# VectorE's copy of the first group's k, ordered ahead of the second pair's reciprocal

## The chip, the cores and the metric
The kernel runs on one core of a Trainium2 chip. The metric is the time of one execution on the device in microseconds (us); less is better.

## What is computed
Three layers follow each other; the changed code is in the first, a gated linear attention over 4 batches, 8 heads, 768 positions and 48 dimensions:

```python
for t in range(S):
    state = alpha[:, :, t, :, None] * state + np.einsum('bhd,bhe->bhde', k[:, :, t], v[:, :, t])
    y[:, :, t] = np.einsum('bhd,bhde->bhe', q[:, :, t], state)
```

Its output, as 3072 tokens of 384 values, goes to a mixture of 8 experts (each token goes to one expert by a greedy order of its logits, at most 384 tokens to an expert; a hidden layer of 1024 with relu), and from there to a gated feed-forward layer of 1536 (`silu(x w_gate) * (x w_val)`, then `w_out`).

## The kernel before
Attention works on four pairs of heads (`p` = 0 to 3). Positions are cut into 12 chunks of 64, and two chunks of a pair make a group, so that a pair has 6 groups and the whole has 24 (`n`; the "first group" is n = 0).

`prep(p)` prepares a pair. It multiplies 32 factors of alpha in a tree (L126, L131, L135; on VectorE for the first two pairs, on GpSimd for the last two), takes the reciprocal of the product (L137), and derives the first factors from it: `rq` (L139), the last slot of g (L142) and the first of f (L143), with a memset of `ab` for the pair after next (L134) beside them. Then a chain of 31 products on VectorE (L166, the "FG steps") fills the tile FG with running factors, eight to a slice. After each slice of eight steps VectorE multiplies them with q (L171) and k (L172). TensorE transposes the results (L187), ScalarE writes them as the high half of q or k (L190), TensorE subtracts that half (L192), and ScalarE writes the low half (L194). So a pair's `qT` and `kT` are complete when the last of its L194 is. The transpose of `ab` (L146) and its copy (L148) give the decay between chunks. FG, qx and kx have one buffer each and are shared by all pairs; `qT` and `kT` have two. The loads of a later pair's q and k (L45) and alpha (L42) go out as soon as the slice before them is used up.

For each group, `sA(n)` copies that group's k from `kT` into one of two buffers `kBD` (two copies on VectorE, L205, one for each head of the pair; of them the change takes the second), starts a DMA on SyncE that transposes it into `kn` (L208), and brings v into halves (L211 on ScalarE, L216 on ScalarE, L217 on GpSimd). `sB` multiplies k with q (L227), masks (L229), subtracts and masks again (L231, L232). `sC` multiplies the transposed k with v (L241) and carries the state from chunk to chunk (L252 on TensorE, L257 on VectorE); it writes the state's two halves (L271 on ScalarE, L272 on GpSimd) and copies v into place (L276 on VectorE). `sD` forms the output (L287), `sE` sends it out (L306 to L313). With two `kBD` buffers, the copy for group n + 2 waits until the transposing DMA and the products of group n have read theirs.

The code is written group by group, but that is not the order on the engines. A scheduler with a timeline of its own places every instruction; `after(a, b)` is the way to tell it that a is to stand behind b. It adds a dependency that only orders, without a semaphore:

```python
    def after(a,b):
        tc.add_manual_dep(a.ins,b.ins.name,mybir.DependencyInfo(mybir.DependencyClass.NoSync,mybir.DependencyReason.DATA),reason="the first pair first")
```

The loads of weights for the last layer are unpacked on VectorE (L655, L657, L659) at the end of attention, in the router and in the first expert. DMAs are issued by SyncE, in order, on eight semaphores in turn, so that each waits for the one issued eight before it.

Of the kernel before, what the change touches and what calls it, by code (L numbers as in the profile page):

```python
# [22 lines left out]
B,H,S,D=4,8,768,48  # L23
# [7 lines left out]
def attention(ctx, tc, q, k, v, alpha, w_gate, xd, RP, MW, side, R):  # L31

    nc=tc.nc
# [24 lines left out]
    def load_v(m):  # L58
        if m>=NP*G//VG: return
        p,w=divmod(m,G//VG)  # L60
        vx[m]=P2.tile([128,VG*GC,B,D],F32,name="vx",tag="vx",bufs=VB)
        for h in range(2):
            for b in range(B):
                nc.sync.dma_start(vx[m][64*h:64*h+64,:,b],
                    bass.AP(tensor=v.tensor,offset=v.offset+(((b//2*2+h)*H+2*p+b%2)*S+w*VG*GC*C)*D,ap=[[D,C],[C*D,VG*GC],[1,D]]))
# [50 lines left out]
            nc.vector.tensor_copy(RI[64*h:64*h+48,48*h:48*h+48],ident[64*h:64*h+48,64*h:64*h+48])  # L116
        cst['wgh']=wgh; cst['RI']=RI

    fq={}
    def after(a,b):  # L120
        tc.add_manual_dep(a.ins,b.ins.name,mybir.DependencyInfo(mybir.DependencyClass.NoSync,mybir.DependencyReason.DATA),reason="the first pair first")
    def prep(p,first=False):
# [6 lines left out]
        n=8  # L129
# [3 lines left out]
        ab=P2.tile([XP,2,64],F32,name="ab")  # L133
        nc.vector.memset(ab,1.0)  # L134
        te.tensor_tensor(ab[:,:,0:D],tr[:,:,0],tr[:,:,1],op=OP.mult); yield  # L135
        inv=P2.tile([XP,2,D],F32,name="inv")
        nc.vector.reciprocal(inv,ab[:,:,0:D])  # L137
        rq=P2.tile([XP,2,D],F32,name="rq")
        nc.vector.tensor_scalar(rq,inv,par[:XP,1:2],par[:XP,0:1],op0=OP.mult,op1=OP.add)  # L139
        f=FG[:,0].rearrange("p j h d -> p h j d")[:,:,:,0:D]  # L140
# [57 lines left out]
    def sA(n):  # L198
        p,g=divmod(n,G)
        kb=kBD[n%NBD]; vb=vBD[n%2]  # L200
        for h in range(2):
            r=slice(64*h,64*h+48)

            o=kb[r].rearrange("p l (b c) h s -> p (l b) c h s",b=B)[:,:,:,h]; x=kT[p][r].rearrange("p l b g c s -> p (l b) g c s")[:,:,g]
            nc.vector.tensor_copy(o,x)  # L205

        kn[n]=P2.tile([128,2,U,128],F16,name="kn")
        nc.sync.dma_start_transpose(kn[n].rearrange("p l u x -> p (l u) x"),kb.rearrange("p l u h s -> p (l u h s)"))  # L208
        if g%VG==0:
            vg=vx[n//VG]  # L210
            ii=nc.scalar.activation(vg,vg,AF.Copy,scale=SX)  # L211
            if VD and p==0: after(ii,chain[0])
        vt=vx[n//VG][:,g%VG*GC:(g%VG+1)*GC].rearrange("p c b d -> p b c d")
        vh[n]=P2.tile([128,2,U,D],F16,name="vh",tag="vh",bufs=3)
        vu=vh[n].rearrange("p l (b c) d -> p l b c d",b=B)
        nc.scalar.activation(vu[:,0],vt,AF.Copy)  # L216
        nc.gpsimd.tensor_tensor(vu[:,1],vt,vu[:,0],op=OP.subtract)  # L217
        if g%VG==VG-1: load_v(n//VG+VB)
        yield
        yield  # L220
# [113 lines left out]
    for _ in prep(0,True): pass  # L334
    late()
    ready=[0]
    def preps():
        for p in range(1,NP):
            yield from prep(p)
            ready[0]=p  # L340
    cur=preps()
    for i in range(-2,NG+2):

        if 0<=i+2<NG:
            while ready[0]<(i+2)//G: next(cur,None)
        gens=[]
        if 0<=i<NG: gens.append((sC(i),6))
        if 0<=i+1<NG: gens.append((sB(i+1),2))
        if 0<=i-1<NG: gens.append((sD(i-1),3))
        if 0<=i-2<NG: gens.append((sE(i-2),3))  # L350
        if 0<=i+2<NG: gens.append((sA(i+2),2))
        if i+2>=PS0: gens.append((take(cur,PW),PW))
        if SIDE and SS<=i+2<SE: gens.append((take(side,SIDE),SIDE))
        merge(gens)
        if i==NG-RC: R.consts()
# [521 lines left out]
def full(tc,q,k,v,alpha,wg,w1,w2,wg2,wv2,wo2,out):  # L877
    nc=tc.nc
    with ExitStack() as top:
        D=top.enter_context(tc.tile_pool(name="dr",bufs=1,space=bass.MemoryType.DRAM))  # L880
        xd=D.tile([24*128,2,384],F16,name="xd")
        PT=top.enter_context(tc.tile_pool(name="rps",bufs=1,space=PS))
        R=Router(top,tc)
        MW=top.enter_context(tc.tile_pool(name="mw",bufs=1))
        M=Moe2Weights(tc,MW,wg2,wv2,wo2)
        side=M.load()
        with ExitStack() as ctx: L=attention(ctx,tc,q,k,v,alpha,wg,xd,PT,MW,side,R)
        with ExitStack() as ctx:
            R.start(ctx,L,PT)
            ffn(ctx,tc,xd,w1,w2,M,MW,out,R,side)  # L890
# [28 lines left out]
```

## Time and profile before

| | us |
|---|---|
| median of 3 runs | 980.42 |
| the three runs | 979.54, 980.69, 980.42 |
| the profiled execution | 981.15 |
| its span, first to last instruction | 979.4 |

| engine | busy us | share of the span |
|---|---|---|
| TensorE, matrix products | 827.0 | 84% |
| VectorE | 678.1 | 69% |
| ScalarE | 413.8 | 42% |
| GpSimd | 328.1 | 33% |

The profile names TensorE PE, VectorE DVE, ScalarE ACT, GpSimd POOL and SyncE SP (SPq where it issues DMAs). A row of a timeline gives the start in us from the span's start, the duration in us, engine, line, operation, tile written and tiles read, the count of instructions merged into the row, and, where the engine was idle before it, for how long and what ended that. Busy shares are averages over stages with different limits; a stage is read from its own rows.

### The profile page before, as it was taken

Reading aid. Unit: us, or ns where it says so; the run is one execution under the profiler, and the core shown is the slowest. Engines: PE = TensorE matmul, PEld = TensorE weight load, DVE = VectorE, ACT = ScalarE, POOL = GpSimd, SP = SyncE. Lnnn points to the kernel's source line nnn. Section 1 sums busy time; section 2 is a strip of 40 time slices with the busy share of each in tenths; the row PEclk is TensorE's granted clock in tenths of the full one; section 3 lists DMA queues with packets and bytes.
Section 4 is the critical chain, followed back from the end, with each engine's and each line's share of the span. In section 5 each row is a group of like instructions: output and inputs, shape, how many; then the busy total and the mean of one; then the engine's idle time right before and its main releaser. Section 6 shows DMA issues by size and latency. Waiting matters only on the chain. (4 is left out here: it accounts for less than half of the span.)

```text
span 979.4 us, 18512 instructions
## 1 busy us (share of the span) xinstructions
PE 827.0 (84%) x7216; PEld 529.9 (54%) x7216; DVE 678.1 (69%) x1856; ACT 413.8 (42%) x768; POOL 328.1 (33%) x308
## 2 busy tenths in 40 slices
PE   1657788877616778889999999999999998999997
PEld 0446567756413444556656656656655664666664
DVE  7869999749798997756865875774884687232130
ACT  5627576776505543432432342251343245332130
POOL 0153534426304544512431350360342246221231
PEclk9769898998855998999999999999999999999999
DMA  9996877879614440700420250070060038000000
GB/s 182 173 168 140 179 151 126 140 152 195 149 44 156 149 129 1 189 14 1 132 71 1 86 117 1 1 194 9 1 181 21 1 123 234 23 1 1 25 1 24
DMA packets 148055, 90.28 MB, mean 92 GB/s; under 512 B 121344, under 2 KB 138752, under 8 KB 147968
## 3 DMA queue, kind: packets, MB, share of 16 engines
q1 hardware_dynamic: 144896, 79.67, 35.5%
q0 software_dynamic: 3072, 9.44, 3.0%
q8 instruction: 56, 0.92, 0.4%
q14 instruction: 31, 0.25, 0.1%
HBM read 62.94 MB, written 9.44 MB: 74 GB/s over the span
## 5 line engine op out<-in xcount | busy, mean ns | idle before, releaser
L805 POOL TENSOR_TENSOR pTa<-pp,pTa 128x384 f16<-128x384 f32 x64 | 59.6, 932 | 258.6 <-ACT pTa L804 258.4
L766 PE MATMUL ph<-xT,w1s 128*128 128x384 f16 x576 | 103.6, 335 | 13.5 <-ACT o L816 10.1
L800 DVE TENSOR_TENSOR sg<-sg,pg 128x384 f32<-128x384 f32 x96 | 52.7, 549 | 77.0 <-ACT sg L799 76.9
L813 PE MATMUL po<-ma,pTa 128*128 128x384 f16 x576 | 104.0, 329 | 2.3 <-ACT pTa L804 2.3
L778 PE MATMUL px<-hT,w2s 128*128 128x384 f16 x576 | 97.0, 326 | 3.3 <-DVE hT L768 1.9
L766 PEld LDWEIGHTS <-w1s 128*128 128x128 f16 x576 | 56.3, 100 | 53.2 <-issue 20.7
L778 PEld LDWEIGHTS <-w2s 128*128 128x128 f16 x576 | 55.8, 98 | 40.0 <-issue 3.8
L796 PEld LDWEIGHTS <-mb 128*128 128x128 f16 x576 | 55.2, 98 | 40.5 <-issue 4.9
L813 PEld LDWEIGHTS <-pTa 128*128 128x128 f16 x576 | 55.6, 98 | 38.7 <-ACT pTa L804 2.4
L796 PEld LDWEIGHTS <-mc 128*128 128x128 f16 x576 | 55.8, 98 | 36.8 <-issue 1.2
L796 PEld LDWEIGHTS <-ma 128*128 128x128 f16 x576 | 55.4, 98 | 35.7
L804 ACT ACTIVATE pTa<-pp 128x384 f16<-128x384 f32 x64 | 33.3, 522 | 88.4 <-DVE pp L803 88.4
L799 ACT ACTIVATE sg<-pg 128x384 f32<-128x384 f32 x96 | 46.6, 486 | 53.1 <-PE pg L796 50.7
L803 DVE SCALAR_TENSOR_TENSOR pp<-sg,pv 128x384 f32<-128x384 f32 x96 | 52.9, 551 | 17.9 <-PE pv L796 13.5
L711 POOL TENSOR_TENSOR w2s<-stage,w2s 128x768 f16<-128x768 f32 x32 | 56.4, 1767 | 24.9 <-ACT stage L710 24.5
L796 PE MATMUL pg<-x,mb 128*128 128x384 f16 x288 | 57.8, 326 | 4.5 <-DVE sg L800 2.5
L805 POOL TENSOR_TENSOR pTb<-pp,pTb 128x384 f16<-128x384 f32 x32 | 30.0, 938 | 87.8 <-ACT pTb L804 87.8
L217 POOL TENSOR_TENSOR vh<-vx,vh 128x384 f16<-128x384 f32 x24 | 24.6, 1030 | 100.4 <-ACT vh L216 82.2
L796 PE MATMUL pv<-x,mb 128*128 128x384 f16 x288 | 57.7, 326 | 0.0
L166 DVE TENSOR_TENSOR FG<-FG,al 96x192 f32<-96x192 f32 x124 | 52.9, 437 | 2.1
L796 PE MATMUL pv<-x,mc 128*128 128x384 f16 x288 | 53.2, 331 | 0.0
L796 PE MATMUL pg<-x,mc 128*128 128x384 f16 x288 | 52.7, 326 | 0.0
(246 smaller groups left out, 1864.9 us busy)
## 6 DMA issues: line engine op xcount, KB each, us to landing
stage<-in_moe_w_dram SPq DMA_DIRECT2D x32, 384.0 KB
stage<-in_moe_w_dram SPq DMA_DIRECT2D x23, 512.0 KB
al<-in_alpha_dram SPq DMA_DIRECT2D x16, 288.0 KB
vx<-in_v_dram SPq DMA_DIRECT2D x64, 72.0 KB
xd<-xr SPq DMA_DIRECT2D x24, 192.0 KB
words<-in_moe_w_gate_dram SPq DMA_DIRECT2D x9, 512.0 KB
words<-in_moe_w_val_dram SPq DMA_DIRECT2D x9, 512.0 KB
words<-in_moe_w_out_dram SPq DMA_DIRECT2D x9, 512.0 KB
```

The costliest lines, as they stand in the source:

```text
L166: chain[p]=nc.vector.tensor_tensor(fg(j,HB-1-j),fg(j-1,HB-j),aa(j,HB-j),op=OP.mult)
L217: nc.gpsimd.tensor_tensor(vu[:,1],vt,vu[:,0],op=OP.subtract)
L711: behind(nc.gpsimd.tensor_tensor(dst[1],s,dst[0],op=OP.subtract),lo_after)
L766: mm(ps,lhsT=a[:,l,k,f*128:(f+1)*128],rhs=x[:,r,k],start=i==0,stop=i==8); i+=1
L778: mm(ps,lhsT=b[:,l,f,d*128:(d+1)*128],rhs=hT[:,r,f],start=i==0,stop=i==23); i+=1
L796: mm(ps,lhsT=w[:,l,k,f%4*128:(f%4+1)*128],rhs=x2[:,r,k],start=i==0,stop=i==8); i+=1
L799: nc.scalar.activation(sg,pg,AF.Sigmoid,scale=2.0**-16)
L800: nc.vector.tensor_tensor(sg,sg,pg,op=OP.mult)
L803: nc.vector.scalar_tensor_tensor(p,sg,2.0**-13,pv,op0=OP.mult,op1=OP.mult)
L804: nc.scalar.activation(pT[e][f//4][:,0,f%4],p,AF.Copy)
L805: nc.gpsimd.tensor_tensor(pT[e][f//4][:,1,f%4],p,pT[e][f//4][:,0,f%4],op=OP.subtract)
L813: mm(po,lhsT=pT[e][f//4][:,l,f%4,t*128:(t+1)*128],rhs=M.o[f//4][:,r,f%4],start=i==0,stop=i==35); i+=1
```

## The change
The copies of `sA` are kept by group number, and the reciprocal of the second pair (p = 1) gets an ordering dependency: it is to stand behind the first group's copy (the second of its two, on the same engine).

```diff
-    fq={}
+    fq={}; kc={}
...
-        nc.vector.reciprocal(inv,ab[:,:,0:D])
+        ri=nc.vector.reciprocal(inv,ab[:,:,0:D])
+        if p==1 and 0 in kc: after(ri,kc[0])
...
-            nc.vector.tensor_copy(o,x)
+            kc[n]=nc.vector.tensor_copy(o,x)
```

Behind line 137 every line number of the changed kernel is one higher. The scheduler places all that follows anew. Three places of that:

VectorE before, from the end of the second pair's tree (L135) to the third group's copy; kBD_135 and kBD_136 are the two buffers, ah are masked products of groups:

```order
L135 TENSOR_TENSOR ab<-tr 96x2x48
L137 RECIPROCAL inv<-ab 96x96
L139 TENSOR_SCALAR rq<-inv,par 96x96
L142 TENSOR_SCALAR FG<-inv,par 96x2x48
L134 MEMSET ab 96x128
L143 TENSOR_TENSOR FG<-al,rq 96x2x48
L205 COPY kBD_135<-kT 48x16x64 x2
L205 COPY kBD_136<-kT 48x16x64 x2
L166 TENSOR_TENSOR FG<-FG,al 96x2x2x48 x3
L229 TENSOR_TENSOR ah<-pA,mask 128x512
L166 TENSOR_TENSOR FG<-FG,al 96x2x2x48 x2
L229 TENSOR_TENSOR ah<-pA,mask 128x512
```

The rows that follow before are one more L166, an L232 and the third group's copy. The same stretch with the change, to the third group's copy:

```order
L206 COPY kBD_135<-kT 48x16x64 x2
L137 RECIPROCAL inv<-ab 96x96
L206 COPY kBD_136<-kT 48x16x64 x2
L140 TENSOR_SCALAR rq<-inv,par 96x96
L143 TENSOR_SCALAR FG<-inv,par 96x2x48
L134 MEMSET ab 96x128
L230 TENSOR_TENSOR ah<-pA,mask 128x512
L144 TENSOR_TENSOR FG<-al,rq 96x2x48
L167 TENSOR_TENSOR FG<-FG,al 96x2x2x48
L230 TENSOR_TENSOR ah<-pA,mask 128x512
L167 TENSOR_TENSOR FG<-FG,al 96x2x2x48
L233 TENSOR_TENSOR ah<-pA,mask 128x512
```

The first group's two copies stand ahead of the reciprocal, the second group's behind it, and two FG steps instead of six stand ahead of the third group's copy.

TensorE before, where the transposes of the second pair's first slice stand (L187; r and pY belong to the groups' output):

```order
L231 LDWEIGHTS negs
L231 MATMUL pA<-ah,negs 128x512
L187 MATMUL pt<-rid,FG 128x96 x8
L293 LDWEIGHTS negs
L293 MATMUL pY<-yh,negs 128x512
```

And with the change, the same transposes (now L188), 162 rows further on:

```order
L288 LDWEIGHTS sBD_140
L288 MATMUL pY<-qT,sBD_140 128x64
L288 LDWEIGHTS sBD_140
L288 MATMUL pY<-qT,sBD_140 128x64
L288 LDWEIGHTS sBD_140
L288 MATMUL pY<-qT,sBD_140 128x64
L188 MATMUL pt<-rid,FG 128x96 x8
```

They have moved behind products of the second group's output, which read that group's state halves (sBD_140).

VectorE before, at the first copies of the second pair (its first two groups):

```order
L276 COPY vBD_138<-vh 64x16x48 x2
L166 TENSOR_TENSOR FG<-FG,al 96x2x2x48 x7
L171 TENSOR_TENSOR FG<-qx,FG 96x2x8x48
L205 COPY kBD_135<-kT 48x16x64 x2
L205 COPY kBD_136<-kT 48x16x64 x2
L172 TENSOR_TENSOR FG<-kx,FG 96x2x8x48
```

And with the change:

```order
L277 COPY vBD_138<-vh 64x16x48 x2
L172 TENSOR_TENSOR FG<-qx,FG 96x2x8x48
L173 TENSOR_TENSOR FG<-kx,FG 96x2x8x48
L167 TENSOR_TENSOR FG<-FG,al 96x2x2x48 x8
L206 COPY kBD_135<-kT 48x16x64 x2
L206 COPY kBD_136<-kT 48x16x64 x2
L172 TENSOR_TENSOR FG<-qx,FG 96x2x8x48
L173 TENSOR_TENSOR FG<-kx,FG 96x2x8x48
```

The product with q that stood directly ahead of the copies now stands directly behind them.

## Rows read from the trace of the kernel before

**Rows 1.** Busy time by stage: stretch, then each engine's us, clock, DMA share, GB/s
```profile
58.00:113.00 55.00, 43.68 (x715) 33.89 (x716) 51.68 (x107) 35.90 (x76) 18.67 (x20) 0.90 0.74 151
113.00:188.00 75.00, 61.40 (x1072) 50.41 (x1071) 71.60 (x130) 49.19 (x102) 35.74 (x34) 0.87 0.80 153
188.00:212.00 24.00, 21.08 (x384) 16.99 (x382) 7.35 (x19) 21.87 (x47) 8.17 (x9) 0.99 0.59 130
...
262.00:312.00 50.00, 17.12 (x138) 10.25 (x139) 44.13 (x188) 9.87 (x15) 11.29 (x12) 0.52 0.29 87
312.00:979.40 667.40, 627.03 (x4050) 375.55 (x4047) 416.02 (x1218) 236.74 (x424) 220.31 (x190) 0.99 0.23 65
...
320.00:340.00 20.00, 13.45 (x90) 7.66 (x89) 19.93 (x37) 11.08 (x20) 11.67 (x9) 1.00 0.48 141
```

**Rows 2.** Timeline of TensorE and ScalarE, the end of the first pair's k
```profile
44.83 0.40 PE L146 MATMUL pt<-rid,ab 96*128 96x96 f32 x1 [1.03 <-DVE ab L135]
45.02 0.85 PE L192 MATMUL pt<-kT,negs 128*128 128x384 f16 x1
...
45.90 0.49 ACT L194 ACTIVATE kT<-pt 128x384 f16<-128x384 f32 x1 [0.39 <-PE pt L192]
```

**Rows 3.** Timeline of VectorE, from the reciprocal to the third group's copy
```profile
44.72 0.75 DVE L137 RECIPROCAL inv<-ab 96x96 f32<-96x96 f32 x1
...
46.43 1.75 DVE L205 COPY kBD<-kT 48x1024 f16<-48x1024 f16 x4
48.20 1.13 DVE L166 TENSOR_TENSOR FG<-FG,al 96x192 f32<-96x192 f32 x3
...
51.11 0.34 DVE L166 TENSOR_TENSOR FG<-FG,al 96x192 f32<-96x192 f32 x1
51.38 0.68 DVE L232 TENSOR_TENSOR ah<-pA,mask 128x512 f16<-128x512 f32 x1
58.14 1.22 DVE L205 COPY kBD<-kT 48x1024 f16<-48x1024 f16 x2 [6.08 <-DMA kn<-kBD]
```

**Rows 4.** Timeline of SyncE, the first transposing DMAs
```profile
47.33 5.15 SPq L64 DMA_DIRECT2D vx<-in_v_dram  x5
52.58 6.15 SPq L208 DMA_TRANSPOSE kn<-kBD  x2
```

**Rows 5.** Timelines of VectorE and GpSimd, 64 to 75 us
```profile
64.61 0.95 DVE L171 TENSOR_TENSOR FG<-qx,FG 96x768 f32<-96x768 f32 x1
...
71.07 0.36 DVE L257 TENSOR_TENSOR st<-pU,gam 112x192 f32<-112x192 f32 x1 [0.70 <-PE pU L252]
72.07 0.69 DVE L232 TENSOR_TENSOR ah<-pA,mask 128x512 f16<-128x512 f32 x1 [0.64 <-PE pA L231]
...
74.74 0.33 DVE L142 TENSOR_SCALAR FG<-inv,par 96x96 f32<-96x96 f32 x1 [0.56 <-PE pt L187]
...
70.66 1.89 POOL L272 TENSOR_TENSOR sBD<-st,sBD 48x384 f16<-48x384 f32 x2 [0.66 <-ACT sBD L271]
```

**Rows 6.** Timeline of ScalarE, VectorE and GpSimd at the second pair's first copies
```profile
111.52 0.49 ACT L194 ACTIVATE kT<-pt 128x384 f16<-128x384 f32 x1 [0.19 <-PE pt L192]
...
112.41 0.95 DVE L171 TENSOR_TENSOR FG<-qx,FG 96x768 f32<-96x768 f32 x1
...
113.29 6.38 DVE L205 COPY kBD<-kT 48x1024 f16<-48x1024 f16 x4
113.32 3.65 POOL L126 TENSOR_TENSOR tr<-al 96x1536 f32<-96x1536 f32 x1 [10.03 <-DMA al<-in_alpha_dram]
...
119.70 1.64 DVE L172 TENSOR_TENSOR FG<-kx,FG 96x768 f32<-96x768 f32 x1
```

**Rows 7.** The tile kBD: durations in ns, least, median and most, of all its copies
```profile
L205 DVE COPY kBD<-kT x48: 406/424/3548, 46.4 to 235.8; 48x1024 f16<-48x1024 f16 x48
```

**Rows 8.** Timeline of VectorE, the last pair's first copies
```profile
211.99 1.75 DVE L205 COPY kBD<-kT 48x1024 f16<-48x1024 f16 x4 [2.08 <-ACT kT L194]
```

**Rows 9.** Groups of VectorE, 44 to 262 us: busy us, mean ns | idle before
```profile
L657 DVE SCALAR_TENSOR_TENSOR w<-words,w 128x512 int32<-128x512 int32 x9 | 8.2, 915 | 0.2
```

## Prediction
> **What bounds the kernel now.** I read the profile from the outside in. First the busy time of each engine by stage [rows 1]. Attention runs to about 262 us. From 58 to 113 us VectorE is busy 51.68 of 55 us and from 113 to 188 us 71.60 of 75, with TensorE (43.68 and 61.40), ScalarE and GpSimd below. From 188 to 212 us VectorE works only 7.35 of 24 us; there ScalarE, with 21.87, turns the last pair's products into q and k. The router that follows attention is VectorE's again (44.13 of 50), in the first expert, 320 to 340 us, VectorE is full once more (19.93 of 20), and over all the rest from 312 us TensorE has 627 of 667 us. So what VectorE loses or saves before 188 us should reach the end, as long as it also moves the start of the last pair's conversion; nothing later gives it back.
>
> Then the place of the change, in the order of time. The copy of the first group's k (L205) reads the first pair's k, whose last piece ScalarE writes (L194) from 45.90 for 0.49 us, to 46.39 [rows 2]. VectorE starts that copy at 46.43 with no idle time shown in front of it; the second pair's reciprocal and the four short operations behind it fill 44.72 to 46.43 [rows 3]. The two agree to 0.04 us: the copy was not held up by the reciprocal in this execution, it came just when its data came.
>
> Then what follows the copy. SyncE issues the transposing DMA of the first group at 52.58, behind five loads of v that start at 47.33 [rows 4]. The copy it reads had ended 5 us earlier (two of the four copies that take 1.75 us from 46.43). What it stood behind is the queue of loads. VectorE ends its last ready operation at 52.06 (51.38 and 0.68) and sits idle 6.08 us, to 58.14, until that transposition lands and frees the buffer for the third group's copy [rows 3]. This is the largest idle time of VectorE in the stage.
>
> **The change part by part.** Beside the two instructions named, the scheduler moves some two hundred rows on VectorE from the first group's copy to the last pair, a second, smaller lot where the router's search and the first expert run side by side, and rows of the other engines with them; no instruction is added or removed.
>
> *The copy in front of the reciprocal.* Gain at most 46.43 − 46.39 = 0.04 us; I take 0. VectorE now idles from 44.72 to 46.4, and the five displaced operations (1.71 us together, 46.43 − 44.72 [rows 3]) run after the copy. Their cover is the 6.08 us idle time. Without that cover they would cost 1.71 us.
>
> *The first transposition.* SyncE's rows are the same up to the third transposition. Two of them, of the fourth and fifth group, then pass the four loads of q and k that stood ahead. These loads serve the third pair, whose FG steps have not begun when they go out, so their delay is hidden. The first transposition stays where it is, behind the loads of v: no gain, no loss. If that cover were gone, the copy would still give at most 0.04 us.
>
> *The steps that leave the shadow.* Before, six of the second pair's FG steps (L166) stood ahead of the copy that waits until 58.14; now two do. Four steps are done after the wait instead of before it. A step that stands alone between other work takes 0.27 us (51.38 − 51.11), one of three in a row 1.13/3 = 0.38 [rows 3]. Most of the moved ones stand alone, so I take 4 × 0.27 = **+1.08 us**, with 1.51 (4 × 0.38) as the other end.
>
> *What the groups gain.* With those steps behind, the first products with q and k (L171 and L172 at 64.61 [rows 5]) drop behind the fifth group's copy, and the groups of the first pair run ahead. VectorE waited three times for TensorE there: 0.70, 0.64 and 0.56 us, 1.90 together [rows 5]. The last one is in front of an L142 that now has eight more operations ahead of it, so I take it as gone. The other two are in front of group work (L257 and L232) that now comes earlier on VectorE, but on TensorE too, since the second pair's transposes (L187) have moved behind it; I take one as gone (0.64) and one as staying. That is **−1.20 us**; the ends are 0 and −1.90.
>
> *The second pair's first copies.* At 112.41 an L171 stood ahead of them and took until 113.29, 0.88 us [rows 6]; now it stands behind. VectorE has to do it anyway, so I take 0; if the earlier start of the second pair's groups shortens a wait later on, it is worth up to −0.88.
>
> The copies there hide a second thing. Four copies took 6.38 us beside a multiply of GpSimd that ran from 113.32 for 3.65 us [rows 6]; the fastest copy takes 0.406 us, the median 0.424, the slowest 3.548 [rows 7]. If the copies come 0.88 us earlier and the multiply, which waits for its load, does not, the copy that took 3.548 could run free: 3.548 − 0.424 = 3.12 us less. By the rows alone that is a gain of 3.1 us.
> The Trainium skill (GPSIMD Engine Reference, section Key points) says that GpSimd shares its SBUF interfaces with VectorE and contends with operations that use two ports or have two inputs in SBUF. By that rule the products L171 and L172, which would then lie beside the multiply, are held in the copies' place, and the sum gets nothing of the 3.1 us. The trace agrees in part: an L172 beside GpSimd's next products took 1.64 us against 0.95 for the same shape before them [rows 6].
> In the sum I put 0, since I cannot see that the load would not come earlier too.
>
> *The rest.* In the last two pairs each group's copy has at most two products or a few short operations more or less ahead of it; I take 0. In the first expert steps of the router's search stand up to four rows from where they stood, behind or ahead of the unpacking of weights (L655 to L659). VectorE is full there, so one such operation on the wrong side costs what it lasts, 0.915 us for the longest kind [rows 9], and it may as well be saved: I take 0, with 0.9 either way.
>
> Sum: 0 + 0 + 1.08 − 1.20 + 0 = **−0.1 us** against the profiled execution's 981.15 us (its span is 979.4 us). That execution is 0.73 us above the median of 980.42, so the forecast is 980.42 − 0.1 = **980.3 us**: no change. The measurement tells about 0.2%, 2 us, from no change. With the ends of the terms (+1.08 − 1.90 − 0.88 − 0.9 = −2.6; +1.51 + 0 + 0 + 0.9 = +2.4) this case alone holds 977.8 to 982.8.
>
> **The rivals.**
> *Faster: the copies slip past GpSimd's multiply.* For it: the 0.88 us; against it: they must be ready, and ScalarE ends the second pair's k only at 112.0 us (111.52 and 0.49 [rows 6]); the start of the multiply hangs on a load that the same reordering may advance, and VectorE's other products may be held instead. Time: 980.3 − 3.1 = 977.2 us; if all four run free (6.38 − 4 × 0.424 = 4.68), 975.6.
>
> *Slower: the second pair's conversion falls behind TensorE's output products.* In the new order the transposes of the second pair's first slice (L187) stand behind the second group's output products (L287), and these need the state halves that GpSimd writes for 1.89 us from 70.66 [rows 5]. VectorE's L143 of the third pair needs those transposes done before it may overwrite FG, and everything on VectorE is queued behind L143. It decides when VectorE reaches L143 before TensorE is through, about 73 us. Then no wait is recovered (0 in place of −1.20), the four steps cost 1.51, and up to 1.89 comes on top: +3.4, or 983.8 us. For it: TensorE now has one more group's products ahead of L187. Against it: VectorE has five more operations ahead of L143, and three waits that existed in this stretch may go.
>
> *The change does what it says.* If ScalarE's last piece of k came earlier, the copy could gain up to 1.71 us, 978.7 us. But ScalarE's and TensorE's rows there are unchanged, and TensorE starts the product for that piece (L192, 45.02) behind a transpose (L146, 44.83) that waits for VectorE's own earlier row [rows 2]; and the transposition would still stand behind the loads.
>
> A later sign that would bear on all of them is the start of the last pair's copies, 211.99, after 2.08 us of waiting for ScalarE [rows 8].
>
> **How the numbers follow.** Forecast 0.50, the slip past the multiply 0.26, the conversion behind 0.21, the change doing what it says 0.03. Faster by over 0.2% is under 978.5, slower over 982.4. Of the forecast's own 0.50, whose ends lie just beyond both, I give 0.03 to faster and 0.02 to slower. So faster is 0.26 + 0.03 = 0.29, slower 0.21 + 0.02 = 0.23, and within 0.2% lies 0.45 + 0.03 = 0.48. The range leaves about one in ten out on each side: it goes through most of the first rival's prices (977.2, at most 975.6) and nearly to the second's (983.8): 976.5 to 983.6 us. The likeliest case's own range is 977.8 to 982.8.
>
> **What would show it.** Right: VectorE's first L205 again near 46.4, now with about 1.7 us of idle time in front and ScalarE's L194 as what ended it; the third group's copy again near 58.1 after an idle time of over 5 us; second pair's first copies within 1.5 us of 113.3; last pair's within 2 of 212; the stages after 262 of the same length. Wrong: a first copy before 46 us, or a first transposition before 52 us, would break the first step; four copies near 113 us in under 3.5 us would be the first rival; an idle time of over 1.5 us on VectorE between 68 and 80 us that TensorE's transposes end, with all stages shifted by 2 us or more, the second.

## The result and the profile after

The changed kernel takes 989.2 us (median of 4 runs, 987.96 to 990.14), the kernel before 979.98 us in the same comparison (4 runs, 978.78 to 980.69). The ratio is 1.0095, with a 95% interval of 1.0077 to 1.0112: slower by 9.2 us. The forecast was 980.3 us, no change, with a range of 976.5 to 983.6. The profiled execution after took 988.42 us, its span is 986.6 us.

First the place of the change. Timelines of VectorE and GpSimd after, from the end of the second pair's tree to the third group's copy (all line numbers behind 137 are one higher), and then of GpSimd before:

```profile
44.00 0.26 DVE L135 TENSOR_TENSOR ab<-tr 96x96 f32<-96x96 f32 x1
45.99 0.86 DVE L206 COPY kBD<-kT 48x1024 f16<-48x1024 f16 x2 [1.74 <-ACT kT L195]
...
50.70 3.18 DVE L167 TENSOR_TENSOR FG<-FG,al 96x192 f32<-96x192 f32 x1
...
56.62 1.22 DVE L206 COPY kBD<-kT 48x1024 f16<-48x1024 f16 x2 [2.14 <-DMA kn<-kBD]
50.25 3.41 POOL L126 TENSOR_TENSOR tr<-al 96x1536 f32<-96x1536 f32 x1 [7.54 <-DVE FG L167]
```

```profile
51.41 3.42 POOL L126 TENSOR_TENSOR tr<-al 96x1536 f32<-96x1536 f32 x1 [8.27 <-DVE ah L229]
```

This is the first step as forecast: 1.74 us of new idle time, ended by ScalarE's last piece of k; from the tree's last product the copy comes 1.99 us later (45.99 − 44.00), as before (46.43 − 44.43). The transposing DMA stays behind the loads of v, 51.43 against 52.58 [rows 4], and the third group's copy still waits for it. The idle time there is 2.14 us instead of 6.08 [rows 3], the copy itself 1.5 us earlier, with its DMA.

Then the second pair's first copies, timelines of VectorE and GpSimd after:

```profile
113.16 1.74 DVE L206 COPY kBD<-kT 48x1024 f16<-48x1024 f16 x4
114.93 4.08 DVE L172 TENSOR_TENSOR FG<-qx,FG 96x768 f32<-96x768 f32 x1
118.93 1.00 DVE L173 TENSOR_TENSOR FG<-kx,FG 96x768 f32<-96x768 f32 x1
114.54 3.66 POOL L126 TENSOR_TENSOR tr<-al 96x1536 f32<-96x1536 f32 x1 [13.02 <-DMA al<-in_alpha_dram]
```

The copies are as early as before (113.16 against 113.29) and now run free, 1.74 us in place of 6.38 [rows 6]: GpSimd's multiply came 1.22 us later (114.54 against 113.32). But the product behind them takes 4.08 us in place of 0.95.

Busy time by stage after, the stretches of [rows 1]:

```profile
58.00:113.00 55.00, 45.72 (x689) 36.28 (x688) 51.54 (x108) 36.18 (x77) 18.10 (x19) 0.82 0.75 143
113.00:188.00 75.00, 57.01 (x1029) 46.00 (x1028) 70.35 (x127) 46.36 (x95) 33.51 (x32) 0.91 0.75 144
188.00:212.00 24.00, 19.11 (x298) 15.20 (x296) 9.79 (x19) 15.63 (x34) 8.60 (x9) 0.86 0.73 150
262.00:312.00 50.00, 16.72 (x233) 11.04 (x231) 44.41 (x180) 10.44 (x21) 6.51 (x9) 0.62 0.30 84
312.00:986.60 674.60, 634.38 (x4086) 379.53 (x4086) 420.79 (x1238) 243.69 (x433) 227.66 (x194) 0.98 0.24 67
```

From 188 to 212 us ScalarE was busy 21.87 of 24 us before; now it is 15.63, with 34 operations in place of 47. The conversion of the last pair starves there. The pair's first copies start at 221.96 us in place of 211.99 [rows 8]. So in these two executions the loss lies between 113 and 222 us.

The same stage from its own start, the end of VectorE's last product with k (187.63 before, 189.43 after), to the last pair's copies: first two windows and the whole of before, then the same of after:

```profile
187.63:191.63 4.00, 4.00 (x91) 3.63 (x89) 1.58 (x4) 2.82 (x7) 0.00 (x0) 0.89 0.45 78
191.63:195.63 4.00, 4.00 (x82) 3.49 (x79) 1.41 (x3) 3.79 (x10) 2.70 (x3) 1.00 0.87 87
187.63:211.99 24.36, 21.44 (x391) 17.35 (x389) 7.60 (x19) 22.10 (x48) 8.17 (x9) 0.98 0.59 129
```

```profile
189.43:193.43 4.00, 1.83 (x34) 1.84 (x35) 2.45 (x5) 0.60 (x2) 1.75 (x2) 0.69 0.78 187
193.43:197.43 4.00, 4.00 (x50) 3.16 (x48) 0.76 (x2) 1.47 (x3) 0.00 (x0) 0.50 0.84 126
189.43:221.96 32.53, 26.73 (x405) 20.90 (x406) 9.78 (x23) 22.16 (x49) 9.90 (x11) 0.84 0.53 109
```

ScalarE does the same work, 22.1 us, in 32.53 instead of 24.36 us. In the first 8 us it gets 2.07 us of work (0.60 + 1.47), before 6.61. TensorE is busy 1.83 of 4 us in the first window and works at a granted clock of 0.50 in the second.

What TensorE waits for stands on VectorE. Timelines of VectorE and TensorE, before and then after:

```profile
182.99 0.68 DVE L232 TENSOR_TENSOR ah<-pA,mask 128x512 f16<-128x512 f32 x1
183.59 1.59 DVE L205 COPY kBD<-kT 48x1024 f16<-48x1024 f16 x2
185.21 1.55 DVE L171 TENSOR_TENSOR FG<-qx,FG 96x768 f32<-96x768 f32 x1
186.69 0.94 DVE L172 TENSOR_TENSOR FG<-kx,FG 96x768 f32<-96x768 f32 x1
185.23 0.61 PE L227 MATMUL pA<-qT,kBD 112*128 112x64 f16 x8 [1.42 <-DVE kBD L205]
```

```profile
186.90 0.94 DVE L172 TENSOR_TENSOR FG<-qx,FG 96x768 f32<-96x768 f32 x1
187.76 1.67 DVE L173 TENSOR_TENSOR FG<-kx,FG 96x768 f32<-96x768 f32 x1
189.36 0.67 DVE L233 TENSOR_TENSOR ah<-pA,mask 128x512 f16<-128x512 f32 x1
189.96 1.58 DVE L206 COPY kBD<-kT 48x1024 f16<-48x1024 f16 x2
191.60 0.61 PE L228 MATMUL pA<-qT,kBD 112*128 112x64 f16 x8 [3.00 <-DVE kBD L206]
```

The last two products of the last pair stand ahead of the masked product of group 15 and the copies of group 17 instead of behind them. And a second row moved, on SyncE; its timeline before and after:

```profile
177.61 5.13 SPq L208 DMA_TRANSPOSE kn<-kBD  x2
182.83 1.04 SPq L313 DMA_DIRECT2D xd<-xr  x1
183.96 5.06 SPq L64 DMA_DIRECT2D vx<-in_v_dram  x7
...
191.99 3.49 SPq L208 DMA_TRANSPOSE kn<-kBD  x1
...
196.23 0.56 SPq L650 DMA_DIRECT2D words<-in_moe_w_gate_dram  x1
```

```profile
182.49 4.95 SPq L209 DMA_TRANSPOSE kn<-kBD  x2
189.46 0.39 SPq L651 DMA_DIRECT2D words<-in_moe_w_gate_dram  x1
189.94 0.83 SPq L314 DMA_DIRECT2D xd<-xr  x1
190.87 5.00 SPq L64 DMA_DIRECT2D vx<-in_v_dram  x7
198.90 3.00 SPq L209 DMA_TRANSPOSE kn<-kBD  x1
```

The first load of weights now stands ahead of an output, seven loads of v and the transposition of group 17. It goes into memory that the last pair's k uses (`words` has the tag of `kx`), so it waits for the last product with k, which ends at 189.43, and what stands behind it on SyncE waits too. The output goes out at 189.94 instead of 182.83, the transposition at 198.90 instead of 191.99. Only some 2 us of that are this wait (187.44 to 189.46): the two transpositions ahead of it end 4.7 us later than before (187.44 against 182.74), and behind the seven loads the transposition of group 17 stands another 3.0 us (195.87 to 198.90), which the profile puts down to TensorE.

### The profile page after: what moved, and what is told of

Read it like the earlier page. It is cut to its first block, busy times and chain, and to the rows that moved or that the text cites. A ratio compares the mean times of both kernels' runs of the same rounds, so it can differ in the third digit from the quotient of the medians.

```text
span 986.6 us, 18516 instructions
## 1 busy us (share of the span) xinstructions
PE 833.9 (85%) x7216; PEld 533.3 (54%) x7216; DVE 681.7 (69%) x1856; ACT 414.9 (42%) x768; POOL 331.6 (34%) x308
## 5 line engine op out<-in xcount | busy, mean ns | idle before, releaser
L767 PE MATMUL ph<-xT,w1s 128*128 128x384 f16 x576 | 101.2, 329 | 11.7 <-ACT o L817 9.0
L779 PE MATMUL px<-hT,w2s 128*128 128x384 f16 x576 | 100.9, 334 | 3.9 <-DVE hT L769 3.8
L806 POOL TENSOR_TENSOR pTb<-pp,pTb 128x384 f16<-128x384 f32 x32 | 30.4, 950 | 86.9 <-ACT pTb L805 86.9
L167 DVE TENSOR_TENSOR FG<-FG,al 96x192 f32<-96x192 f32 x124 | 57.7, 478 | 2.1
L273 POOL TENSOR_TENSOR sBD<-st,sBD 48x384 f16<-48x384 f32 x46 | 48.4, 1052 | 27.7 <-ACT sBD L272 22.7
```

The costliest lines, as they stand in the source:

```text
L167: chain[p]=nc.vector.tensor_tensor(fg(j,HB-1-j),fg(j-1,HB-j),aa(j,HB-j),op=OP.mult)
L273: (nc.vector if n>=NG-ND else nc.gpsimd).tensor_tensor(sb[r,1,:,h,0:D],s[r],sb[r,0,:,h,0:D],op=OP.subtract)
L767: mm(ps,lhsT=a[:,l,k,f*128:(f+1)*128],rhs=x[:,r,k],start=i==0,stop=i==8); i+=1
L779: mm(ps,lhsT=b[:,l,f,d*128:(d+1)*128],rhs=hT[:,r,f],start=i==0,stop=i==23); i+=1
L806: nc.gpsimd.tensor_tensor(pT[e][f//4][:,1,f%4],p,pT[e][f//4][:,0,f%4],op=OP.subtract)
```

## The experiments

**The instrument.** One dependency makes the scheduler place everything anew. To undo single rows, each kernel writes out the whole order of all five engines:

```diff
         full(tc, *args)
+        pin(tc)
...
+def pin(tc):
+    t={i.name:i for i in tc.nc.cur_bb.bb.instructions}
+    for row in PIN.values():
...
+        for a,b in zip(s[1:],s):
+            tc.add_manual_dep(t[a],b,mybir.DependencyInfo(mybir.DependencyClass.NoSync,mybir.DependencyReason.DATA),reason="order")
```

`PIN` lists the instructions of each engine. The traces of `old_both` and `words_back` show the order before, and after, on all five engines but for the rows moved. A mixed order is made by `hybrid`: up to a time in one kernel's trace its rows, then the remaining rows as the other has them. The diffs below show, in shorthand, only what `PIN` holds. All are built on the kernel before and have its line numbers. Executions of one kernel spread by some 10 us (before: 975.9 to 988.1 in 30), so intervals are 0.2 to 0.3% to each side (2 to 3 us), and the stage lengths of the profiled executions, one for each kernel, are read beside them. Differences in us are of the medians; the ratio is worked out otherwise and can be 1 to 2 us off them.

**Where the loss lies.**

```diff
+PIN=hybrid([('new',113.15),('old',None)])
```


> Every engine keeps the changed kernel's order up to the start of the second pair's first copies (113 us, where the two executions stand level: 113.29 before, 113.16 after the change) and from there the order of the kernel before. Theory A, that the loss lies in the rows the scheduler re-placed behind that point: the time is that of the kernel before within 1 us. Theory B, that the new front itself (first copy, reciprocal, the groups that run ahead) leaves something late that only shows later: about 9 us slower, as the change.

983.27 against 980.22 us, ratio 1.0026 (1.0004 to 1.0049): 3 us, between the two theories.

```diff
+PIN=hybrid([('old',113.28),('new',None)])
```


> The mirror of the run above: the order of the kernel before up to the second pair's first copies, the changed kernel's order from there on. Theory A: 8 to 10 us slower than before, although the place of the change is as it was. Theory B: within 1 us of before.

987.89 against 980.22, 1.0061 (1.0041 to 1.0081): 7.7 us by the medians, 6 by the ratio. Most of the loss comes with rows behind 113 us, a smaller part with the front.

```diff
+PIN=hybrid([('new',191.5),('old',None)])
```


> The changed kernel's order up to the end of VectorE's products of the last pair (191.5 us in its trace), then the order of the kernel before. The stage from the second pair's copies to there took 4.0 us longer after the change (78.4 against 74.3 us), the stage from there to the last pair's copies 6.0 us longer (30.4 against 24.4). Theory C, that the two stages lose on their own: about 4 us slower than before. Theory D, that the second stage is only slow because the first one is late: 8 to 10 us slower.

989.96 against 980.22, 1.0087 (1.0057 to 1.0117): the time that theory D gave. The order behind 191 us makes no difference that shows; the slow stage (31.4 us in this run) is decided by rows ahead of it.

```diff
 L135 TENSOR_TENSOR ab<-tr
+L205 COPY kBD_135<-kT x2
 L137 RECIPROCAL inv<-ab
+L205 COPY kBD_136<-kT x2
 L139 TENSOR_SCALAR rq<-inv,par
...
-L205 COPY kBD_135<-kT x2
-L205 COPY kBD_136<-kT x2
```


> The order of the kernel before on all engines, but for the place of the change alone: on VectorE the first group's two copies stand ahead of the second pair's reciprocal, the second group's two copies directly behind it, and the rq, g, memset and f operations behind those. Theory A: no change, within 1 us, since the 6.08 us idle time ahead of the third group's copy takes the 1.7 us up. Theory B: it loses several us.

980.57 against 980.22, 1.0000 (0.9979 to 1.0020). The change in its own place costs nothing beyond the noise of 2 us.

**Which stretch.**

```diff
+PIN=hybrid([('old',113.28),('new',152.6),('old',None)])
```


> The order of the kernel before on all engines, but between the second pair's first copies (113 us) and the third pair's (153 us) the changed kernel's order. Theory E: the loss comes from there, because the state steps of groups 8 to 11 (L257) fall behind more factor steps and products, so that the second pair's last output, and with it the start of the last pair's conversion, comes about 5 us later (64 instead of 59 us after the second pair's first copies): 5 to 8 us slower than before. Theory F, that the loss lies in the rows from 153 to 191 us: within 1 us of before.

982.9 against 981.28, 1.0028 (1.0006 to 1.0050). The start of the conversion (the last pair's first L190) came 60.8 us behind the second pair's copies instead of 59.0, but the profiled execution ended attention no later than before. The loss is small, 0.6 to 4.9 us, below the 5 to 8 of theory E.

```diff
+PIN=hybrid([('old',153.15),('new',191.5),('old',None)])
```


> The order of the kernel before, but between the third pair's first copies (153 us) and the end of VectorE's products of the last pair (191 us in the changed kernel) the changed kernel's order. Theory E: within 2 us of before, since the state steps of groups 8 to 11 come in time. Theory F: 5 to 8 us slower, with the copy of the third pair's last group (n = 17) behind the last products as in the changed kernel, about 37 us behind the pair's first copy instead of 30.

987.26 against 981.28, 1.0058 (1.0033 to 1.0082): 6 us, as theory F has it. The copy of group 17 came 33.9 us behind the pair's first instead of 30.4. (The profiled execution, 981.06 us, was this kernel's fastest; its stage lengths are a lower end.)

```diff
 L276 COPY vBD<-vh x2
 L166 TENSOR_TENSOR FG<-FG,al
 L257 TENSOR_TENSOR st<-pU,gam
+L205 COPY kBD<-kT x2
 L171 TENSOR_TENSOR FG<-qx,FG
 L172 TENSOR_TENSOR FG<-kx,FG
 L232 TENSOR_TENSOR ah<-pA,mask
-L205 COPY kBD<-kT x2
```


> The changed kernel's order on all engines, but on VectorE the two copies of group 17 (189.96 us there) stand ahead of the three operations directly ahead of them: the last products with q and k and a masked product. In the changed kernel's trace TensorE stood still for 3.00 us until these copies (to 191.60) and then worked at a granted clock of 0.50 to 195 us and 0.65 to 199. Theory G, that this stop and the low clock behind it lose 3 to 4 us of the 9: about 5.5 us slower than before instead of 9, the stage from there to the last pair's copies 3 us shorter. Rival: ScalarE's and TensorE's conversion is late anyhow, and the time stays within 1 us of the changed kernel's.

989.34 against 981.28, 1.0091 (1.0058 to 1.0124): nothing gained, though the copies started at 185.4. TensorE's timeline shows why:

```profile
190.73 0.96 PE L227 MATMUL pA<-qT,kBD 112*128 112x64 f16 x15 [3.59 <-DVE ah L232]
```

The same matmuls now waited for the masked product, which had stayed behind the products. The run moved half of what was needed; it tells nothing against theory G.

```diff
-L171 TENSOR_TENSOR FG<-qx,FG
-L172 TENSOR_TENSOR FG<-kx,FG
-L166 TENSOR_TENSOR FG<-FG,al
 L257 TENSOR_TENSOR st<-pU,gam
+L171 TENSOR_TENSOR FG<-qx,FG
+L172 TENSOR_TENSOR FG<-kx,FG
+L166 TENSOR_TENSOR FG<-FG,al
```
(one of ten such moves)

> The order of the kernel before, but between 137 and 188 us ten state steps (L257, groups 7 to 14) are moved up on VectorE by 0.5 to 2.6 us, ahead of factor steps, products and v copies that stood ahead of them although TensorE's part had been done. If the place of the state steps among the factor steps decides when the last pair's conversion starts, as theory E has it, this gains 1 to 3 us over the kernel before. If VectorE's total work alone decides: no change.

981.69 against 981.28, 0.9997 (0.9969 to 1.0025): no change. An earlier start of the conversion (57.5 in place of 59.0 us behind the copies) gains nothing clear of the noise; with `mid1_new` nothing is left that speaks for theory E, though a gain of 1 to 2 us could hide here.

**The two rows.** For last_prod, mid2_prod, prod_words, mid2_both and three_undone on VectorE:

```diff
-L171 TENSOR_TENSOR FG<-qx,FG
-L172 TENSOR_TENSOR FG<-kx,FG
 L232 TENSOR_TENSOR ah<-pA,mask
 L205 COPY kBD<-kT x2
+L171 TENSOR_TENSOR FG<-qx,FG
+L172 TENSOR_TENSOR FG<-kx,FG
```


> The changed kernel's order on all engines, but on VectorE the last pair's last products with q and k (L171, L172) stand behind the masked product of group 15 and the copies of group 17 instead of ahead of the three, as in the kernel before. In the changed kernel TensorE stood still for 3.00 us until those copies and then worked at half clock; with the copies alone moved up it stood still for 3.59 us until the masked product. Theory G: with both in front, TensorE waits under 1.5 us, the clock stays near 1.00 and the stage from the products to the last pair's copies shrinks from 33 to 25 to 28 us: 3 to 6 us faster than the changed kernel, 3 to 6 slower than before. Rival: the conversion's start, 5 us late, decides: within 1 us of the changed kernel.

990.02 against 981.63, 1.0094 (1.0064 to 1.0124): no gain in the time. The stage shrank only to 29.4 us. TensorE's first stop was gone (0.79 us), and later ones took its place; TensorE and SyncE in that run:

```profile
202.82 0.47 PE L241 MATMUL pU<-vh,kn 128*128 128x48 f16 x12 [1.84 <-DMA kn<-kBD]
207.18 0.90 PE L187 MATMUL pt<-rid,FG 96*128 96x96 f32 x4 [3.48 <-ACT qT L194]
```

```profile
191.20 0.38 SPq L650 DMA_DIRECT2D words<-in_moe_w_gate_dram  x1
...
198.20 1.69 SPq L208 DMA_TRANSPOSE kn<-kBD  x1
```

Later products make the load of weights later (191.20), and here the transposition follows the load, the output and the seven loads of v without a pause.

> The run with the changed order between 153 and 191 us alone, with the same two products moved behind the masked product and the copies. Theory G: 0 to 2 us slower than before instead of 6. Rival: as without the move, 5 to 7 us slower.

987.07 against 981.63, 1.0073 (1.0041 to 1.0105), stage 28.6 us: the rival, for the same reason (TensorE waited 2.26 us for `kn`, until 198.94). This led to theory J. On SyncE, for the next three and for three_undone:

```diff
-L650 DMA words<-in_moe_w_gate_dram
 L313 DMA xd<-xr
 L64 DMA vx<-in_v_dram x7
...
 L64 DMA vx<-in_v_dram
+L650 DMA words<-in_moe_w_gate_dram
```


> The changed kernel's order on all engines, but on SyncE the first load of weights (L650, into the memory of the last pair's k) stands behind the last load of v again, as in the kernel before, instead of ahead of an output DMA, seven loads of v and the transposition of group 17. In the changed kernel SyncE issued it at 189.46 us, at the end of the last product with k (189.43), and the transposition at 198.90. Theory J, that this wait on SyncE is one of two stops of the last conversion, the other the copies of group 17 behind the last products: alone it returns little, 0 to 3 us, since the other stop stays. Rival K, that SyncE's place does not matter: within 1 us of the changed kernel, and the same with both undone.

988.97 against 980.63, 1.0091 (1.0072 to 1.0111), stage 31.6 us: alone it returns nothing that shows.

> The changed kernel's order with both undone: the load of weights back behind the loads of v, and the last products behind the masked product of group 15 and the copies of group 17. Theory J: the stage from the last product to the last pair's copies falls from 32.5 us to 24 to 26, and the time to 2 to 5 us slower than before instead of 9. Rival K: 8 to 10 us slower, as with the products alone moved.

986.62 against 980.63, 1.0070 (1.0050 to 1.0089), 6.0 us slower: 2 to 3 of the 9 us are back (2.4 us by the medians against `words_back`, where the products stand ahead), a little less than theory J had it. The stage has its old length again; its first 4 us and the whole of it, and then TensorE's timeline at its seam:

```profile
193.09:197.09 4.00, 4.00 (x76) 3.40 (x73) 2.63 (x7) 3.48 (x9) 0.68 (x1) 1.00 0.65 121
193.09:217.41 24.32, 20.09 (x351) 15.59 (x348) 7.60 (x20) 20.40 (x46) 8.14 (x9) 1.00 0.59 132
```

```profile
190.69 0.64 PE L227 MATMUL pA<-qT,kBD 112*128 112x64 f16 x16 [0.79 <-DVE kBD L205]
```

24.32 us, with the clock at 1.00 throughout and a wait of 0.79 us. The stage ahead of it, though, from the third pair's first copies to the last product, takes 39.1 us (after 36.7, before 34.4). Some of that only moved from one stage into the other, since the last product, from which the stage is counted, now stands behind three more rows. From the third pair's first copies to the last pair's it is 69.3 us after, 63.4 here and 58.8 before.

> The order of the kernel before with the changed order between 153 and 191 us alone, and in that both undone. Theory J: within 2 us of before (the stretch alone was 6 us slower, with the products moved 7 us, the stage behind the last product 28.8 and 28.6 us; here 24 to 26). Rival K: 5 to 7 us slower.

982.83 against 980.63, 1.0033 (1.0006 to 1.0059), stage 26.0 us: 2.2 us by the medians (3.2 by the ratio) in place of 6. That is close to theory J's 2 us; the intervals of `mid2_new` and `mid2_both` overlap.

```diff
 L257 TENSOR_TENSOR st<-pU,gam
...
+L171 TENSOR_TENSOR FG<-qx,FG
+L172 TENSOR_TENSOR FG<-kx,FG
 L232 TENSOR_TENSOR ah<-pA,mask
 L205 COPY kBD<-kT x2
-L171 TENSOR_TENSOR FG<-qx,FG
-L172 TENSOR_TENSOR FG<-kx,FG
```
```diff
+L650 DMA words<-in_moe_w_gate_dram
 L313 DMA xd<-xr
 L64 DMA vx<-in_v_dram x7
...
-L650 DMA words<-in_moe_w_gate_dram
```


> The order of the kernel before on all engines, with only these two put in: the first load of weights ahead of the output DMA of group 11 on SyncE, and the last products with q and k ahead of the masked product of group 15 and the copies of group 17 on VectorE. Theory J: 3 to 7 us slower than before, the stage behind the last product 27 us or more. Rival K: within 1.5 us.

985.16 against 980.63, 1.0051 (1.0030 to 1.0072): 4.5 us, as theory J said. TensorE's stop and SyncE's load in the timeline of this kernel, and then the window of the whole stage:

```profile
184.56 0.93 PE L227 MATMUL pA<-qT,kBD 112*128 112x64 f16 x24 [3.99 <-DVE kBD L205]
182.42 0.39 SPq L650 DMA_DIRECT2D words<-in_moe_w_gate_dram  x1
```

```profile
182.39:212.70 30.31, 25.30 (x421) 20.33 (x422) 9.79 (x24) 22.76 (x49) 9.91 (x11) 0.89 0.59 117
```

Three moved rows make the stage 30.31 us where it was 24.36, in part because the product from which it is counted now stands ahead of three rows; from the third pair's first copies to the last pair's it is 61.8 us against 58.8. Neither the load nor the products were put into the old order alone, so this run does not tell how the two share the loss.

**The rest of it.**

```diff
 L232 TENSOR_TENSOR ah<-pA,mask
+L166 TENSOR_TENSOR FG<-FG,al x4
 L205 COPY kBD<-kT x2
...
-L166 TENSOR_TENSOR FG<-FG,al x4
```
(on the order of new113_old; the four stood singly behind the copy)

> The run with the changed kernel's order up to 113 us and the old one behind (3 us slower than before), with the next four factor steps moved up ahead of the third group's copy, where VectorE idles. Theory H, that the front loses because these steps left the idle time: the stretch from the third group's copy to the second pair's first copies shrinks by 1.1 to 1.5 us, from 56.6 to 57.9 us in three executions, and the time is 1 to 2 us slower than before. Rival: other rows of the front lose; the stretch stays above 56.5 us.

982.09 against 981.63 (median of 11 executions), 1.0014 (0.9992 to 1.0037). The time would fit theory H, but its interval overlaps that of `new113_old`. The stretch stayed at 57.0 us in the one profiled execution, which speaks against H. VectorE had no idle time left to hide the steps in:

```profile
49.54 3.25 DVE L166 TENSOR_TENSOR FG<-FG,al 96x192 f32<-96x192 f32 x1
...
53.31 3.77 DVE L166 TENSOR_TENSOR FG<-FG,al 96x192 f32<-96x192 f32 x4
57.01 1.55 DVE L205 COPY kBD<-kT 48x1024 f16<-48x1024 f16 x2
```

One step lasted 3.25 us beside GpSimd's multiply for the third pair.

```diff
+PIN=hybrid([('new',113.15),('old',153.15),('new',None)])
```
(with the products and the load moved as above)

> The changed kernel's order with three things undone: the load of weights back behind the loads of v, the last products behind the masked product and the copies, and the order from the second to the third pair's first copies (113 to 153 us) as in the kernel before. With the first two alone the time was 6.0 us above before. Theory L, that the rest is what the front loses (3 us with the new front alone) and what the order of 113 to 153 us pushes behind 153 us (five of VectorE's rows fewer done by then): 2 to 4 us slower than before. Rival: the rows behind 153 us lose on their own, 5 to 7 us slower.

985.26 against 980.88, 1.0042 (1.0017 to 1.0066): 4.4 us, just outside theory L's 2 to 4. The order between 113 and 153 us may be worth some of it (the stage behind falls from 39.1 to 36.5 us), but the interval overlaps that of `prod_words`. The split between it, the front and the rows behind 153 us stays open.

**A version that beats both.** VectorE idles in the conversion stage, so work without a due time can go there. For `fill` also `pin` of the unpacking, which would forbid the move, is taken out:

```diff
-        if self.after is None: return self.tc.keep_in_program_order(ins)
+        if self.after is None: return ins
...
+L655 TENSOR_SCALAR w<-words
+L657 SCALAR_TENSOR_TENSOR w<-words,w
+L659 SCALAR_TENSOR_TENSOR w<-words,w
...
 L276 COPY vBD<-vh x2
 L205 COPY kBD<-kT x4
```


> The order of the kernel before, but nine unpacking operations (three tiles of weights, L655 to L659, 5.4 us together) stand ahead of VectorE's v copy at 209.19 us instead of behind the last pair's first copies. VectorE waits for TensorE and ScalarE for 5.93 us there, and the weights were issued by 197.3 us. If VectorE's work bounds the stage from 212 to 262 us, this gains 2 to 5 us over the kernel before; if TensorE's or the transposing DMA's chain does, under 1 us.

979.82 against 981.63, 0.9976 (0.9954 to 0.9997): faster by about 2 us, at the low end of the expectation. From the last pair's copies to the end of attention it took 48.0 us (50.2 before).

```diff
-                    if (p>=LE and jj//4%LM==0) or (first and j0>=EJ): nc.vector.tensor_scalar(Tv[:,1,:,jj:jj+4],pv,SX,None,op0=OP.mult)
+                    if (p==3 and (w,jj) in ((1,12),(0,24),(0,28),(1,0),(1,4))) or (first and j0>=EJ): nc.vector.tensor_scalar(Tv[:,1,:,jj:jj+4],pv,SX,None,op0=OP.mult)
```


> The order of the kernel before with the nine unpacking operations in VectorE's idle time as in fill, and five of the last pair's sixteen low halves (L194, the last five that ScalarE writes, at 204.4 to 211.4 us) written by VectorE instead of ScalarE, in the same idle time. ScalarE was busy 22.1 of the 24.4 us of that stage, so this takes 2.4 us from it. If ScalarE bounds the stage: 1 to 3 us faster than fill (which was 0.24% faster than before), 3 to 5 us faster than before. If TensorE does, or VectorE's operations now wait for each other: as fill or slower.

979.41 against 980.88, 0.9976 (0.9958 to 0.9995): as fill. The stage stayed at 24.0 us although ScalarE was busy only 19.1 us of it (21.9 in `fill`), so ScalarE's time alone does not set it. What does was not tried.

## Why the prediction was wrong

- **The copy, the reciprocal, the first transposition**: right. No gain, no loss, shown by the trace after and by `local` (1.0000).
- **The 6.08 us of cover**: right in what it covers, wrong in size. GpSimd's multiply for the third pair, which before ran mostly in that idle time (51.4 to 54.8 us), now starts at 50.25, beside VectorE's steps, and stretches one to 3.18 us; 2.14 us of idle time were left.
- **The steps and the groups' waits, +1.08 − 1.20**: from the third group's copy to the second pair's the new order takes 56.3 us (mean of eight profiled executions, 54.8 to 57.9), the old 54.9 (eleven, 54.0 to 56.6). So +1.4 us in place of −0.1, inside the ends given. The two profiles stand level at 113 us only because the third group's copy, which waits for the transposing DMA, started 1.5 us later in the one before (58.1 against 56.6; 56.0 to 59.4 in the others).
- **The multiply of GpSimd**: the copies did slip past it, because it came 1.22 us later and not because they came earlier; yet L171 (now L172) took 4.08 us. The reading of the Trainium skill's rule (GPSIMD Engine Reference, section Key points) had been that the trace agrees in part and the sum stays at 0. By that rule, which names the interfaces that GpSimd shares with VectorE, the products are held in the copies' place; the trace after agrees (4.08 us). The faster rival fell with it.
- **The slower rival**: the sign, not the place. L144 after shows no wait; at 66.53 us a state step waits 1.37 us for output products, no more than the three waits that went.
- **"The rest ... I take 0"**: the step that failed. I had looked at VectorE's copies in the last two pairs and judged a displacement of "at most two products" by what such a row lasts. The rows behind the second pair's first copies, which no other term prices, cost 6 to 8 us when they alone are the changed kernel's (`old113_new`). Part of it is shown row by row: the cost is set by who waits. Three TensorE waits were read where VectorE is the bound, but at the seam to the next stage, where TensorE and ScalarE carry the work, two products ahead of a masked product and a copy held TensorE for 3.00 us, and its granted clock read 0.50 behind that. And SyncE was compared only as far as the third transposition; the load of weights that moved ahead of an output and seven loads was not looked at. The two together are worth 2 to 3 us in the changed order and 4.5 us put into the old one.
- **The other 6 to 7 us** are not settled to the row, and their cause stays open. The front has some 1.4 to 3; VectorE's rows between the third pair's copies and the last product grew from 67 to 72 in the windows of prod_words (busy 32.7 to 37.3 us), which would be work that the new order left undone by 153 us; `three_undone`, which puts that stretch back, gains too little to show it.

A late sign had been named: the last pair's copies at 211.99. They came 10 us later. That nothing behind gives it back was not quite right: the span of the same execution is 7.2 us longer (986.6 against 979.4), so some 3 us were made up behind the copies. The medians differ by 9.2.

## What to carry to other kernels

When a dependency goes to a scheduler, its own place may matter least: compare the whole order, on the DMA queue as well, and look first at the seams, where the engine that is full hands over to another. There a row is priced by who waits for it, not by how long it lasts. A load into reused memory is better issued behind the transfers that need not wait for the memory's last reader. When one stop is removed and the time stays, look for the next one behind it before the theory is dropped: here neither of two moves gave anything back alone that showed, and both together gave 2 to 3 us.

## What the runs showed of the hardware

- An f32 step or product of VectorE that met a GpSimd multiply of 96x1536 (3.4 to 3.7 us) lasted about as long as what was left of the multiply: a step of 0.34 us took 3.18 (GpSimd from 50.25 to 53.66 us, the step from 50.70 to 53.88), a product of 0.95 us 4.08. The Trainium skill (Trainium Architecture — The Big Picture, section What this means for kernel authors) calls the shared port an exclusive lock and no split of bandwidth; these rows agree, and the f16 copy of 3.548 us [rows 7] fits them. Not every operation was held: before, the masked product at 51.38 [rows 3], which takes one of its inputs from TensorE's result `pA`, kept its 0.68 us beside the multiply that started at 51.41.
- Behind the stop of 3.0 us on TensorE the granted clock read 0.50, the lower level of 1.2 GHz, from 193.4 to 197.4 us, and ScalarE got 1.47 us of work in those 4. No run shows what the stop alone is worth in the time. With the load of weights back, moving the two products, which cut it to 0.79 us, gave some 2 us (988.97 to 986.62, `words_back` to `prod_words`).
- One load that was not ready held SyncE's queue: nothing was issued from 187.44 to 189.46 us, and the output and the seven loads behind it then went out in a row (189.94 to 195.87). With the load moved back (`prod_words`) output and loads followed the transpositions after 0.9 us. The Trainium skill (DMA: Bandwidth & Descriptors, section Anatomy of one DMA — SWDGE (gpsimd) path) has it, for DMAs that GpSimd issues, that DMA engines do not wait and that a wait is made on the issuing sequencer before dispatch; SyncE's rows at 189.46 and 189.94 agree.
